# Sliding-window attention and an S4 convolution: x read flat and first, pools on two sides with waits by tile, projections dealt over the real table steps, the kernel's transform beside the first maxima

## The chip, the core and the metric

One core of one Trainium2 chip runs the whole program. The metric is the time of one execution on the device in microseconds (us); the time of a kernel is the median of its runs. The engines are PE (matrix multiplication, with PEld for its weight loads), DVE (vector), ACT (activation functions), POOL (the second vector-like engine) and SP, which here only issues DMA transfers. Each engine runs its own list of instructions in order and waits on semaphores for the others.

## What is computed

```python
def _A_ref(x, wqkv, wo):              # x 1x2048x576, 32 heads of 18
    qkv = (x @ wqkv).reshape(B, S, 3, H, Dh).transpose(2, 0, 3, 1, 4)
    q, k, v = qkv[0], qkv[1], qkv[2]
    scores = einsum("bhqd,bhkd->bhqk", q, k) * Dh ** -0.5
    scores = where(0 <= i - j < 256, scores, -1e9)
    o = einsum("bhqk,bhkd->bhqd", softmax(scores), v)
    return o.transpose(0, 2, 1, 3).reshape(B, S, D) @ wo

def _B_ref(u, A_re, A_im, B_re, B_im, C_re, C_im, log_dt, Dskip):
    P = exp(dt * A * l)               # 576 channels, 128 states, l = 0..2047
    K = einsum("dn,dnl,dn->dl", Cc, P, dB).real
    return causal_convolution(u, K) + u * Dskip

out = concatenate([_A_ref(...), _B_ref(...)], axis=-1)
```

## The kernel before

Two independent halves share the engines. Their work is cut into generators, and `merge` takes from several of them in proportion to the numbers given with them.

**Up to the seam** the Tile framework orders the instructions by itself, from the order in which they are written. `proj` first reads x in eight pieces of 512 KB and the weights `wqkv` in four, for the largest absolute value of each (`amax`), which sets a power-of-two scale. Then it cuts the weights into two float16 parts (`wh`, `wl`), reads x a second time in four chunks of 512 tokens, cuts each likewise (`xh`, `xl`), and makes 13 steps per chunk: nine blocks of q and k (14 matmuls of 512 columns each, evicted to `qst` and stored to the DRAM tensor `qd`) and four steps of v (28 matmuls of 288 columns, stored to `vd`). With the steps for loads and weights that is 16 and 56 steps. All projection matmuls carry line 172 in the profile of before.

`s4_prep` multiplies the S4 parameters by dt and splits two of them into three bfloat16 parts each (`split3`). `tables` builds the convolution kernel K (64 x 128 x 144 values) in 36 half-steps of 16 channels: exponentials (`mg`, `mab`), sines (`fraction`, `qtable`), products on POOL (`m`), and then the taps, 128 small matmuls into `kp` (line 418), evicted to K every second half-step (line 424, 18 times). It has 308 steps after the first 20. `s1_u` is the first stage of the convolution's transform for u, 16 blocks, each stored to `gx` in two transfers of 288 KB (matmuls on line 461, evictions on lines 128 and 130 by `evac`, three of four on ACT and the fourth on DVE).

**The seam.** When all of this is done, `s1_k` runs the same first stage over K: eight blocks of 1152 columns, each stored to `gk` in two transfers of 576 KB, from two buffers `g1`. Then the pools of the second half are opened, `att_setup` clears the operand sets on DVE, and two units of Q and K are loaded.

**After the seam** the order is written out by hand (`manual_schedule`). `attention` first makes the row maxima of unit 0 (`gmax(0)`, 19 steps, matmuls on line 636, maxima on line 643), together with six steps of the convolution `conv`. The maxima go back by a small DMA (`Q<-mt`), and then come 96 items: scores (line 677), exponentials (line 679), masks on POOL (line 688), values (line 700), with the maxima of the next unit, steps of `conv` (95 over the 76 items from the third on, 17 over the next 16), and later the output projection (line 903). `conv` starts with the load of its first operands (`tx` from `gx`, `tk` from `gk`); its matmuls are on lines 500 and 508. SP's queue takes nearly all loads and stores, in order.

## Time and profile before

| | |
|---|---|
| times of the runs | 1076.2, 1079.5, 1081.78 us, median 1079.5 |
| the profiled execution | 1075.61 us, its span 1073.6 us |
| PE busy | 857.8 us, 80% of the span |
| DVE busy | 736.2 us, 69% |
| ACT busy | 619.9 us, 58% |
| POOL busy | 511.1 us, 48% |
| moved by DMA | 152.27 MB, mean 142 GB/s |

The span runs from the first to the last instruction. A row of the profile for a group of instructions gives the source line, the engine, the operation, what it writes and reads by the program's names, the shapes and the count, then the busy time in us and the mean ns of one, and then the engine's idle time before these instructions with what ended most of it. In a row of the timeline the first number is the start in us from the start of the span and the second the duration; the brackets behind it hold the idle time before and what ended it. A matmul of float32 operands leaves two records per instruction.

### The profile page before, as it was taken

Reading aid. Unit: us, or ns where it says so; the run is one execution under the profiler, and the core shown is the slowest. Engines: PE = TensorE matmul, PEld = TensorE weight load, DVE = VectorE, ACT = ScalarE, POOL = GpSimd, SP = SyncE. Lnnn points to the kernel's source line nnn. Section 1 sums busy time; section 2 is a strip of 40 time slices with the busy share of each in tenths; the row PEclk is TensorE's granted clock in tenths of the full one; section 3 lists DMA queues with packets and bytes.
Section 4 is the critical chain, followed back from the end, with each engine's and each line's share of the span. In section 5 each row is a group of like instructions: output and inputs, shape, how many; then the busy total and the mean of one; then the engine's idle time right before and its main releaser. Section 6 shows DMA issues by size and latency. Waiting matters only on the chain.

```text
span 1073.6 us, 26801 instructions
## 1 busy us (share of the span) xinstructions
PE 857.8 (80%) x10332; PEld 450.7 (42%) x10332; DVE 736.2 (69%) x1859; ACT 619.9 (58%) x955; POOL 511.1 (48%) x606
## 2 busy tenths in 40 slices
PE   1535879897988797987578888878888899988787
PEld 0313436554744464553234333333333344434345
DVE  2879685669576845226676788888878766767564
ACT  1776758776797784233146655566566656644471
POOL 0004344435452632010235677766876666666770
PEclk9966989998998998999889999999999999999999
DMA  9665423442344232588616456454645644579763
GB/s 271 168 184 160 105 53 88 109 94 59 85 111 96 55 74 64 130 217 239 188 49 180 138 147 175 147 148 127 176 113 177 185 118 142 146 185 256 204 190 121
DMA packets 155911, 152.27 MB, mean 142 GB/s; under 512 B 36856, under 2 KB 134392, under 8 KB 155592
## 3 DMA queue, kind: packets, MB, share of 16 engines
q1 hardware_dynamic: 148152, 131.98, 45.3%
q0 software_dynamic: 6128, 14.60, 5.4%
q10 hardware_dynamic: 1504, 3.99, 1.3%
q8 instruction: 81, 1.33, 0.6%
q14 instruction: 46, 0.38, 0.1%
HBM read 89.12 MB, written 61.01 MB: 140 GB/s over the span
## 4 chain that ended last, share of the span: by engine, by line
PE 37%; DVE 25%; ACT 10%; DMA 10%; issue 9%; POOL 5%; SPq 2%; DVEq 0%; ACTq 0%; POOLq 0%
PE pp L172 8%; PE r L636 4%; PE po L700 4%; PE r L903 4%; PE r L500 4%; PE kp L418 4%; PE pp L461 3%; DVE jk L643 3%; POOL P L688 2%; DMA gk<-g 2%; PE ST L677 2%; PE x L314 2%; PE r L508 2%; DVE tr L358 2%; ACT P L679 2%
## 5 line engine op out<-in xcount | busy, mean ns | idle before, releaser
L643 DVE CUSTOM_DVE_ANT_0 jk<-r,bias 128x288 f32<-128x288 f32 (+7 forms) x512 | 198.0, 433 | 88.7 <-PE r L636 88.0
L679 ACT ACTIVATE P<-ST,esc 128x1024 f32<-128x1024 f32 (+1 forms) x192 | 202.0, 1059 | 92.9 <-PE ST L677 92.1
L380 POOL TENSOR_TENSOR m<-A,tr 128x1024 f32<-128x1024 f32 x72 | 149.5, 2098 | 194.2 <-PE kp L418 139.1
L688 POOL TENSOR_SCALAR_AFFINE_SELECT P<-P 128x512 f32<-128x512 f32 x240 | 171.7, 745 | 103.2 <-ACT P L679 100.8
L636 PE MATMUL r<-K,qb 128*64 128x288 f16 (+7 forms) x1024 | 130.5, 297 | 36.7 <-DVE qb L627 10.7
L700 PE MATMUL po<-P,V 128*32 128x256 f32 (+2 forms) x1408 | 100.2, 395 | 17.5 <-POOL P L688 8.1
L418 PE MATMUL kp<-Q,m 128*32 128x64 f32 x4608 | 88.3, 230 | 27.6 <-DVE Q L401 10.0
L636 PEld LDWEIGHTS <-qb 128*64 128x64 f16 x1024 | 60.3, 109 | 119.3 <-issue 65.6
L536 POOL TENSOR_TENSOR Y<-t,t 64x288 f32<-64x288 f32 x64 | 53.5, 835 | 109.8 <-DVE t L531 107.8
L418 PEld LDWEIGHTS kp<-Q,m 128*32 128x32 f32 x4608 | 75.2, 116 | 56.3 <-issue 41.7
L461 PE MATMUL pp<-ut,w 128*128 128x288 f32 x128 | 52.8, 538 | 40.9 <-DMA ut<-in_u_dram 18.6
L677 PE MATMUL ST<-Q,K 64*128 64x384 f16 (+2 forms) x704 | 73.5, 280 | 3.0 <-DMA Q<-mt 2.9
L237 DVE SCALAR_TENSOR_TENSOR qst<-pp,qst 128x512 f16<-128x512 f32 x36 | 24.7, 685 | 64.7 <-ACT qst L236 61.8
L128 ACT ACTIVATE g<-pp 128x288 f32<-128x288 f32 (+1 forms) x84 | 34.5, 447 | 40.4 <-DMA gk<-g 22.0
L700 PEld LDWEIGHTS po<-P,V 128*32 128x32 f32 x1408 | 35.7, 110 | 52.5 <-issue 25.7
L537 POOL TENSOR_TENSOR Y<-t,t 64x288 f32<-64x288 f32 x64 | 54.5, 852 | 3.8
L461 PEld LDWEIGHTS pp<-ut,w 128*128 128x128 f32 x128 | 28.9, 245 | 61.1 <-issue 24.1
L326 ACT ACTIVATE ab<-k 128x512 f32<-128x512 f32 (+1 forms) x54 | 31.9, 590 | 37.0 <-DVE k L325 36.6
L172 PE MATMUL pp<-xh,wh 128*128 128x512 f16 x180 | 47.9, 388 | 1.2 <-DVE xh L229 1.2
L172 PEld LDWEIGHTS <-wh 128*128 128x128 f16 x324 | 32.0, 101 | 39.3 <-issue 6.6
L172 PE MATMUL pp<-xh,wl 128*128 128x512 f16 x180 | 48.3, 392 | 0.0
L500 PE MATMUL r<-tx,w 128*64 128x288 f32 x256 | 40.2, 430 | 9.9 <-DMA tx<-gx 8.7
(177 smaller groups left out, 1756.1 us busy)
## 6 DMA issues: line engine op xcount, KB each, us to landing
gx<-g SPq DMA_DIRECT2D x32, 288.0 KB
qd<-qst SPq DMA_DIRECT2D x72, 128.0 KB
gk<-g SPq DMA_DIRECT2D x16, 576.0 KB
tx<-gx SPq DMA_DIRECT2D x16, 576.0 KB
tk<-gk SPq DMA_DIRECT2D x16, 576.0 KB
h<-ho SPq DMA_DIRECT2D x16, 576.0 KB
raw<-in_xT_dram SPq DMA_DIRECT2D x16, 512.0 KB
Q<-qd SPq DMA_DIRECT2D x32, 216.0 KB
```

Of the source, the lines that this page charges most:

```text
L172: self.nc.tensor.matmul(ps, u, v, start=(i == 0), stop=(i == len(ops) - 1))
L380: self.nc.gpsimd.tensor_tensor(m, A[:, ch, a0:a0 + 8].unsqueeze(3).to_broadcast(sh), tr[:, ch, part, 0:8].unsqueeze(2).to_broadcast(sh), o ...
L418: nc.tensor.matmul(kp[32 * st:32 * st + 32, c % 2 * JJ2 + j, :], m[:, ch, a0:a0 + 32], Q[:, ch, term % 2, :], start=(term == 0), stop=(ter ...
L461: nc.tensor.matmul(ps, self.w1[:, part, :], src[:, o:o + k], start=True, stop=True)
L500: nc.tensor.matmul(ps[64 * par:64 * par + 64], w2[:, par, 64 * part:64 * part + 64], t[:, 2 * hs:2 * hs + 2, par, :], start=True, stop=True)
L537: nc.gpsimd.tensor_tensor(Y[par][64:128], t1[sl, 1], t2[sl, 1], op=OP.add)
L636: nc.tensor.matmul(ps[64 * b:64 * b + 64, :n], self.qb[:, b, t, :], d["K"][:, b, k0:k0 + n], start=True, stop=True, skip_group_check=True)
L643: nc.vector.tensor_tensor_reduce(out=jk[:, :n], in0=ps[:, :n], in1=self.bias[:, 288 - n:], scale=1.0, scalar=-3e38, op0=OP.add, op1=OP.max ...
L677: nc.tensor.matmul(ps[:, u, o:o + n], d["K"][h, jp, k0:k0 + 128], d["Q"][h, jp, q0:q0 + n], start=True, stop=True, skip_group_check=True)
L679: nc.scalar.activation(pt[:, 2 * jp:2 * jp + 2, lo:hi], ps[:, :, lo:hi], AF.Exp, scale=self.esc)
L688: nc.gpsimd.affine_select(v, v, pattern=[[0, 4], [sg, 128]], compare_op=OP.is_ge, fill=0.0, base=-1 if far else 0, channel_multiplier=-sg)
L700: nc.tensor.matmul(self.po[32 * j:32 * j + 32, t0 * 128:t1 * 128], V[:, kb * 76 + 19 * j:kb * 76 + 19 * j + 32], pt[:, j, o:o + (t1 - t0) ...
```

## The change

Five things, at these places:

- `proj` reads x for its maximum as one flat array, 128 partitions of contiguous rows, in four pieces of 2160 columns and one of 576, into the buffers that later hold `wh`, `wl` and `qst`. These reads and the four of the weights, with their nine maxima, are now its first step, and `build` takes that step before `s4_prep`.
- `pool` places each on-chip pool on a side (left by default, right for K, `s1s`, `pps` and the pools of `proj` and `s1_u`), and asks for waits by tile (`reuse_waits="tile"`) where memory is used again.
- The projections are merged against 308 table steps instead of 400; the first merge takes four projection, 16 table and two u steps.
- `s1_k` makes 16 blocks of 576 columns instead of eight of 1152. Ten are written out with the first half, six beside `gmax(0)`, before the pools of the second half are opened.
- `conv` gives way once after its first load, which is issued in the first item; the six steps that ran beside `gmax(0)` join the others: 101 over the 76 items.

```diff
--- before.py
+++ after.py
@@ -118,8 +118,10 @@
             if d[0] <= n:
                 d[1](*d[2])
 
-    def pool(self, es, name, bufs, space=None):
+    def pool(self, es, name, bufs, space=None, side="left"):
         kw = {} if space is None else {"space": space}
+        if space != DRAM:
+            kw.update(side=side, reuse_waits="tile")
         self.p[name] = es.enter_context(self.tc.tile_pool(name=name, bufs=bufs, **kw))
 
     def evac(self, out, in_):
@@ -159,7 +161,7 @@
         return self.pow2_of(self.pow2_max(parts, nm)[1], nm)
 
     def amax(self, out, v):
-        self.nc.vector.tensor_reduce(out, v, axis=AX.XY, op=OP.max, apply_absolute_value=True)
+        self.nc.vector.tensor_reduce(out, v, axis=AX.XY if len(v.shape) > 2 else AX.X, op=OP.max, apply_absolute_value=True)
 
     def mm14(self, ps, w, x, wsl, xsl, flip=False):
         wh, wl = w
@@ -183,21 +185,25 @@
         nc, a, wp, dp, sp = self.nc, self.a, self.p["wq"], self.p["dram"], self.p["const"]
         self.qd = dp.tile([64 * 54 + 18, L], F16, name="qd")
         self.vd = dp.tile([8, 128, 16, 76], F32, name="vd")
-        amx = sp.tile([128, 12], F32, name="amx")
+        amx = sp.tile([128, 9], F32, name="amx")
         wr = self.p["K"].tile([128, 5, 1728], F32, name="K")
-        for c in range(8):
-            t = self.p["raw"].tile([128, 5, 256], F32, name="raw")
-            self.load_rows(t, a["xT"], slice(c * 256, c * 256 + 256))
-            self.amax(amx[:, c:c + 1], t)
-            if c % 2 == 0:
-                cs = slice(c // 2 * 432, c // 2 * 432 + 432)
-                self.load_rows(wr[:, :, cs], a["wqkv"], cs)
-            yield
+        flat = a["xT"].rearrange("r c -> (r c)").rearrange("(p n) -> p n", p=128)
+        for i, nm in enumerate(("wh", "wl")):
+            t = wp.tile([128, 4320], F32, name=nm)
+            for c in range(2):
+                o = 2160 * (2 * i + c)
+                nc.sync.dma_start(t[:, 2160 * c:2160 * c + 2160], flat[:, o:o + 2160])
+                self.amax(amx[:, 2 * i + c:2 * i + c + 1], t[:, 2160 * c:2160 * c + 2160])
+        t = self.p["pst"].tile([128, 576], F32, name="qst")
+        nc.sync.dma_start(t, flat[:, 8640:])
+        self.amax(amx[:, 4:5], t)
         for c in range(4):
-            self.amax(amx[:, 8 + c:9 + c], wr[:, :, c * 432:c * 432 + 432])
-            yield
-        px, self.sx = self.pow2_scale(amx[:, 0:8], "x")
-        pw, self.sw = self.pow2_scale(amx[:, 8:12], "w")
+            cs = slice(c * 432, c * 432 + 432)
+            self.load_rows(wr[:, :, cs], a["wqkv"], cs)
+            self.amax(amx[:, 5 + c:6 + c], wr[:, :, cs])
+        yield
+        px, self.sx = self.pow2_scale(amx[:, 0:5], "x")
+        pw, self.sw = self.pow2_scale(amx[:, 5:9], "w")
         pz = self.pz = sp.tile([128, 1], F32, name="pz")
         self.esc = sp.tile([128, 1], F32, name="esc")
         nc.vector.scalar_tensor_tensor(pz, px, 0.25, pw, op0=OP.mult, op1=OP.mult)
@@ -471,10 +477,10 @@
             self.s1(ut.rearrange("p l j -> p (l j)"), self.gx, l0, 4, "pps")
             yield
 
-    def s1_k(self):
+    def s1_k(self, pp):
         kf = self.K.rearrange("p l j -> p (l j)")
-        for b in range(8):
-            self.s1(kf[:, b * 1152:(b + 1) * 1152], self.gk, 8 * b, 8, "s1p")
+        for b in range(16):
+            self.s1(kf[:, b * 576:(b + 1) * 576], self.gk, 4 * b, 4, pp[0])
             yield
 
     def conv(self):
@@ -513,6 +519,7 @@
                 self.after(1, nc.sync.dma_start, self.h.rearrange("a l f d -> (a l) f d")[:, 2 * fp:2 * fp + 2, :], ho)
 
         nx = load(0)
+        yield
         last = None
         for fp in range(16):
             cu = nx
@@ -766,18 +773,21 @@
             nc.gpsimd.dma_start(self.od[:, f0:f0 + 18, HQ * hf:HQ * hf + HQ].rearrange("a p n -> p a n"),
                                 h[32 * j:32 * j + 18])
 
-    def attention(self, conv):
-
-
-        self.V, self.Pt, self.osb, self.ops, self.hl, norms = {}, {}, {}, {}, {}, []
+    def attention_start(self):
+        self.V, self.Pt, self.osb, self.ops, self.hl = {}, {}, {}, {}, {}
         self.load_unit(0)
         self.load_unit(1)
-        merge((self.gmax(0), 19), (part(conv, 6), 6))
-        self.begin(1)
+
+    def attention(self, conv):
+
+
+        norms = []
         items = [(i, c, b) for i in range(16) for c in range(2) for b in range(3)]
         wo0, wo1, wo2, wl, self.acc, self.h7 = self.wo_first(), self.wo_part(), self.wo_rest(2), self.wo_load(), [], {}
         for n in range(len(items) + 2):
             self.begin(n)
+            if n == 0:
+                next(conv)
             streams = []
             if n < len(items):
                 i, k = n // 6, n % 6
@@ -804,7 +814,7 @@
                     streams.append((part(gm, g), g))
             if n >= 2:
                 streams.append((self.values(*items[n - 2]), 1))
-                k = share(n - 2, 95, 76) if n < 78 else share(n - 78, 16, 17) if n < 95 else 0
+                k = share(n - 2, 101, 76) if n < 78 else share(n - 78, 16, 17) if n < 95 else 0
                 streams.append((part(conv, k), k))
             if 20 <= n < 52 and n % 2 == 0:
                 next(wl, 0)
@@ -952,39 +962,46 @@
             self.gx = dp.tile([2, 64, 128, 144], F32, name="gx")
             self.gk = dp.tile([2, 64, 128, 144], F32, name="gk")
             self.h = dp.tile([2, 64, 32, D], F32, name="h")
-            with ExitStack() as ek:
-                self.pool(ek, "K", 1)
-                with ExitStack() as e1:
-                    for n, b, s in (("s4c", 1, None), ("pps", 3, PSUM), ("xps", 2, PSUM), ("trig", 1, PSUM),
-                                    ("kps", 1, PSUM)):
-                        self.pool(e1, n, b, s)
-                    with ExitStack() as e2:
-                        self.pool(e2, "prep", 1)
-                        self.s4_prep()
-                    for n, b in (("wq", 1), ("raw", 2), ("x", 1), ("pst", 2), ("s1u", 2), ("s1s", 2), ("ab", 2), ("abt", 1), ("mab", 3),
-                                 ("mg", 4), ("fr", 2), ("Q", 2), ("P", 2)):
-                        self.pool(e1, n, b)
-                    proj, tables, s1u = self.proj(), self.tables(), self.s1_u()
-                    merge((part(proj, 16), 16), (part(tables, 20), 20), (part(s1u, 4), 4))
-                    merge((proj, 56), (tables, 400), (s1u, 12))
-                with ExitStack() as e1:
-                    self.pool(e1, "s1s", 2)
-                    self.pool(e1, "s1p", 3, PSUM)
-                    for _ in self.s1_k():
-                        pass
+            ek, e0 = ExitStack(), ExitStack()
+            self.pool(ek, "K", 1, side="right")
+            self.pool(ek, "s1s", 2, side="right")
+            self.pool(ek, "pps", 3, PSUM, side="right")
+            pp = ["pps"]
+            s1k = self.s1_k(pp)
             with ExitStack() as e1:
-                self.pool(e1, "fc", 1)
+                for n, b in (("s1u", 2), ("wq", 1), ("raw", 2), ("x", 1), ("pst", 2)):
+                    self.pool(e1, n, b, side="right")
+                for n, b, s in (("s4c", 1, None), ("xps", 2, PSUM), ("trig", 1, PSUM), ("kps", 1, PSUM)):
+                    self.pool(e1, n, b, s)
+                proj, tables, s1u = self.proj(), self.tables(), self.s1_u()
+                next(proj)
+                with ExitStack() as e2:
+                    self.pool(e2, "prep", 1)
+                    self.s4_prep()
+                for n, b in (("ab", 2), ("abt", 1), ("mab", 3), ("mg", 4), ("fr", 2), ("Q", 2), ("P", 2)):
+                    self.pool(e1, n, b)
+                merge((part(proj, 4), 4), (part(tables, 16), 16), (part(s1u, 2), 2))
+                merge((proj, 56), (tables, 308), (s1u, 14))
+                for _ in part(s1k, 10):
+                    pass
+            for n, b, s in (("att", 1, None), ("m", 2, None), ("v", 4, None), ("ring", 3, PSUM)):
+                self.pool(e0, n, b, s)
+            self.att_setup()
+            with self.tc.manual_schedule():
+                self.attention_start()
+                merge((self.gmax(0), 19), (s1k, 6))
+                self.begin(1)
+                ek.close()
+                for n, b, s in (("P", 4, None), ("o", 3, None), ("n", 2, None), ("n1", 1, None), ("h7", 1, None),
+                                ("wo", 1, None), ("wo2", 2, None),
+                                ("fc", 1, None), ("fs", 2, None), ("fy", 2, None), ("stp", 2, PSUM), ("ops", 1, PSUM)):
+                    self.pool(e0, n, b, s)
                 self.i2 = self.p["fc"].tile([128, 64], F32, name="i2")
                 nc.sync.dma_start(self.i2, a["c_i2"])
                 self.dsk = self.p["fc"].tile([128, D], F32, name="dsk")
                 nc.sync.dma_start(self.dsk, a["dsk"].partition_broadcast(128))
-                for n, b, s in (("fs", 2, None), ("fy", 2, None), ("att", 1, None), ("m", 2, None), ("P", 4, None),
-                                ("v", 4, None), ("o", 3, None), ("n", 2, None), ("n1", 1, None), ("h7", 1, None), ("wo", 1, None), ("wo2", 2, None),
-                                ("stp", 2, PSUM), ("ops", 1, PSUM), ("ring", 3, PSUM)):
-                    self.pool(e1, n, b, s)
-                self.att_setup()
-                with self.tc.manual_schedule():
-                    self.attention(self.conv())
+                self.attention(self.conv())
+            e0.close()
 
 
 def kernel(**inputs):
```

The lists of instructions are as follows. On DVE, at the program's start, before (`nA_re` is the first S4 operand, `amx` a maximum, `res` the rest of a split):

```order
L288 MEMSET halfpi 128x1
L162 TENSOR_REDUCE amx<-K 128x1 x2
L292 TENSOR_TENSOR nA_re<-nA_re,dtn 96x2304
L294 SCALAR_TENSOR_TENSOR nA_im<-nA_im,dtn 96x2304
L261 TENSOR_TENSOR res<-nA_re,al 96x2304
L298 TENSOR_TENSOR in_B_re<-in_B_re,dt 128x576
```

and now (`wh`, `wl` and `qst` hold pieces of x here):

```order
L294 MEMSET halfpi 128x1
L164 TENSOR_REDUCE amx<-wh 128x1 x2
L164 TENSOR_REDUCE amx<-wl 128x1 x2
L164 TENSOR_REDUCE amx<-qst 128x1
L298 TENSOR_TENSOR nA_re<-nA_re,dtn 96x2304
L164 TENSOR_REDUCE amx<-K 128x1
L267 TENSOR_TENSOR res<-nA_re,al 96x2304
```

The five maxima of x stand ahead of the first S4 operation, and the four over K are spread between the operations of the first split, the last two ahead of its second half.

On PE, at the seam, before (`pp` a projection or first-stage result, `r` with `tx` the convolution's second stage, `r` with `qb` the maxima):

```order
L172 MATMUL pp<-wh,xl 128x288
L172 LDWEIGHTS xl
L172 MATMUL pp<-wh,xl 128x288
L461 MATMUL pp<-K,w_62 128x384 x48
L500 MATMUL r<-tx,w_6125 64x288 x4
L636 LDWEIGHTS qb
L636 MATMUL r<-K_6085,qb 64x32
```

and now:

```order
L424 MATMUL kp<-Q,m_5537 32x64 x8
L424 MATMUL kp<-Q,m_5539 32x64 x8
L467 MATMUL pp<-K,w_62 128x288 x44
L643 LDWEIGHTS qb
L643 MATMUL r<-K_5991,qb 64x32
```

Before, the last taps were followed by 238 projection matmuls and eight of u, and the whole of K's first stage came before the first `r`. Now the last taps stand directly ahead of K's first stage, 44 of whose 64 matmuls (eleven blocks) come before the first maxima; the other five blocks stand between them, four matmuls after every twelve. Over the whole first half 56 projection matmuls now stand ahead of the first taps and 896 between the first and the last, where 714 stood; of u's 64 it is 13 ahead and 51 between, where it was 20, 36 and eight behind.

## The prediction

> **What bounds the kernel now.** I read the times first, then busy time by stretch, then single lines inside the stretches, then the chain of waits at the seams. The page shows no engine above 80% of the span, so the limit has to be looked for by stage. The row of each stretch gives its length, then for each engine the busy time and the number of instructions, the granted TensorE clock, the DMA share and GB/s:
>
> ```profile
> core 0: us, PE busy (x) PEld busy (x) DVE busy (x) ACT busy (x) POOL busy (x), PEclk, DMA share, GB/s
> 0.00:27.00 27.00, 4.54 (x8) 2.35 (x8) 7.32 (x5) 2.96 (x6) 0.91 (x5) 1.00 0.97 271
> 27.00:49.00 22.00, 13.60 (x28) 7.41 (x29) 20.09 (x18) 16.25 (x16) 0.00 (x0) 1.00 0.71 191
> 49.00:91.00 42.00, 12.88 (x34) 4.99 (x32) 33.74 (x40) 31.71 (x41) 9.94 (x7) 0.64 0.62 180
> 91.00:420.00 329.00, 276.64 (x5526) 171.46 (x5527) 230.59 (x347) 242.85 (x412) 141.47 (x69) 0.92 0.36 85
> 420.00:467.70 47.70, 46.00 (x269) 26.06 (x257) 7.12 (x11) 11.72 (x24) 1.45 (x4) 1.00 0.59 131
> 467.70:515.00 47.30, 35.59 (x96) 17.61 (x96) 27.88 (x28) 16.36 (x36) 3.51 (x1) 0.96 0.84 239
> 515.00:543.50 28.50, 16.09 (x109) 7.76 (x110) 19.14 (x79) 4.57 (x9) 6.93 (x10) 0.80 0.47 141
> 543.50:1073.60 530.10, 452.50 (x4278) 213.02 (x4277) 390.31 (x1336) 293.52 (x412) 346.89 (x510) 0.98 0.56 158
> ```
>
> Until 27 us the DMA engines are full. From 27 to 91 DVE and ACT prepare the tables. From 91 to 420, the table stretch, PE is busy for 276.6 of 329 us. From 420 to 467.7 PE works almost alone. To 515 the kernel K goes through its first transform and out to HBM, with DMA at 0.84. Up to 543.5 the first maxima run with six steps of the convolution, and then the attention items start, with PE at 85%.
>
> Who works alone from 420 on is seen from line 172 (projections) and then line 461 (first transforms) in the two stretches:
>
> ```profile
> 91.00:420.00 329.00, 143.22 (x714) 70.11 (x714) 0.92 0.36 85
> 420.00:467.70 47.70, 41.57 (x238) 23.21 (x238) 1.00 0.59 131
> ```
>
> ```profile
> 91.00:420.00 329.00, 25.74 (x72) 14.23 (x72) 0.92 0.36 85
> 420.00:467.70 47.70, 4.75 (x17) 2.78 (x17) 1.00 0.59 131
> ```
>
> A quarter of the projection (238 of 952 matmuls) is left when the tables end: `merge` dealt 56 projection steps against 400 table steps, and the tables have 308.
>
> **The change part by part.** The sum is made on the profiled execution: 1075.6 us around a span of 1073.6. That is 3.9 us under the median of the runs shown, so the same difference is put on the median of 1079.5 at the end.
>
> *The tail goes.* The built order has no projection behind the last taps. The last eviction of K and its predecessors stand here (first and last start):
>
> ```profile
> L424 ACT ACTIVATE K<-kp x18: 1016/1032/1063, 102.9 to 420.3; 128x512 f32<-128x512 f32 x18
> ```
>
> From 420.3 to 467.7 is 47.4 us. Term: -47.4.
>
> *The work comes back inside the tables.* By the built order 896 projection matmuls now stand between first and last taps instead of 714, 56 stand ahead (free: PE idles for 29 of the 42 us before 91), and 51 first-transform matmuls of u instead of 36, at two records each. At the tail's prices that adds 182 x 41.57/238 = 31.8 us and 30 x 4.75/17 = 8.4 us, so 316.8 us of PE in a stretch that was 329 long. It fits, but only at 96%. How dense PE gets there:
>
> ```profile
> 170.00:209.40 39.40, 37.91 (x803) 25.74 (x800) 27.21 (x45) 34.06 (x65) 19.72 (x11) 1.00 0.48 119
> 209.40:222.60 13.20, 9.33 (x212) 6.30 (x213) 11.63 (x20) 6.08 (x12) 5.51 (x3) 0.74 0.24 52
> 275.20:327.90 52.70, 48.46 (x1155) 32.08 (x1156) 39.68 (x63) 43.45 (x78) 29.45 (x14) 1.00 0.39 96
> ```
>
> Over 40 us it reaches 96%, over 53 us 92%; I take 92%, the longer one: 316.8/0.92 = 344, term +15. Ends: 0 if all of it is hidden in the 52 us of PE idle time, -13 if the clock helps as well, +56 if none of the waits shrinks (both worked out as rivals).
>
> The middle row has PE at 9.3 of 13.2 us and a granted clock of 0.74; its dense neighbours have 1.00. Over the whole stretch 0.92 stands for some 53 us at half speed. The Trainium skill (TensorE: Matmul & The Clock Gate, HAM oscillation) says that PE idle gaps beyond about 3.4 us let the clock fall to half; by that rule a fuller stretch would lose such spells, and the term would be -13 (rival e).
>
> *x first.* x is now read once flat, ahead of everything on SP's queue, and once more in pieces for the transform's operands. ACT's own loads run beside it, and their rows and those of the table's start are:
>
> ```profile
> 22.31 0.62 ACTq L286 DMA_DIRECT2D in_C_im<-in_p_C_im_dram  x1
> 22.97 1.28 ACT L289 ACT_TABLE_LOAD   x1 [22.97 <-DMA dt<-in_ldt_dram]
> 24.51 2.56 DVE L292 TENSOR_TENSOR nA_re<-nA_re,dtn 96x2304 f32<-96x2304 f32 x1
> 47.78 2.39 DVE L162 TENSOR_REDUCE amx<-K 128x1 f32<-128x2160 f32 x1
> 71.08 0.55 DVE L325 TENSOR_TENSOR k<-x,k 128x384 f32<-128x384 f32 x1
> ```
>
> ```profile
> q10 hardware_dynamic: 1504, 3.99, 1.3%
> ```
>
> x is 576 x 2048 x 4 bytes = 4.72 MB; with ACT's 3.99 MB (q10), 8.7 MB at the first row's 271 GB/s are in at 32 us, and DVE's `nA_re`, now queued behind five maxima of x, starts there instead of at 24.5. The weights (4.42 MB) follow until 48.5, so the last maximum over K is where it was, 47.8. But behind it in line now stand what used to run earlier (the second halves of both splits, four products by dt) and what came later (four weight conversions, two of x, evictions). By these rows the waiting ACT and DVE pieces are:
>
> ```profile
> L162 DVE TENSOR_REDUCE amx<-raw 128x1 f32<-128x1280 f32 x7 | 10.3, 1480 | 1.1 <-DMA raw<-in_xT_dram 0.9
> L209 ACT ACTIVATE wh<-K,wr 128x2160 f16<-128x2160 f32 x4 | 8.4, 2091 | 0.0
> L264 DVE TENSOR_TENSOR res<-res,al 32x2304 f32<-32x2304 f32 x1 | 2.5, 2550 | 0.5 <-ACT al L263 0.5
> ```
>
> ```profile
> 31.93 0.75 DVE L298 TENSOR_TENSOR in_B_re<-in_B_re,dt 128x576 f32<-128x576 f32 x1
> ```
>
> After 51: 8.1 us on DVE (2.55 + 2.5 for the second split + 3.0 for the products), then on ACT two conversions of that split, one more, and four of weights (3 x 2.1 + 4 x 2.1 = 14.7), some 9 of small evictions, and 2.7 for x: the first fraction k comes near 86 instead of 71.1. From there to the first taps, which the chain has at 91.28, the old order needed 20.2 us, of which five maxima of x (7.4) and one weight pass (2.5) are gone: 86 + 10.3 = 96. Term +5, with +1 for projections now in ACT's line: +6. Ends: -4 (the 9.9 us of removed maxima and weight pass as pure gain, less 6 for x landing later) and +20 (a rival).
>
> ```profile
> 91.28 3.43 PE kp L418 x120
> ```
>
> *The seam.* K's first transform is now 16 blocks with stores of 288 KB instead of 8 with 576 KB, still in two buffers. How long a buffer is held, one eviction pair of u, the wait for tx, the maxima, and the wait for their result:
>
> ```profile
> 473.58 0.37 SPq L463 DMA_DIRECT2D gk<-g  x1
> ...
> 477.18 0.87 ACT L128 ACTIVATE g<-pp 128x384 f32<-128x384 f32 x2 [2.09 <-DMA gk<-g]
> ```
>
> ```profile
> 450.28 0.90 ACT L128 ACTIVATE g<-pp 128x288 f32<-128x288 f32 x2 [1.47 <-PE pp L461]
> ```
>
> ```profile
> 515.26 6.09 DMA tx<-gx
> ...
> 542.33 1.72 DMA Q<-mt
> ```
>
> ```profile
> L643 DVE CUSTOM_DVE_ANT_0 jk<-r,bias 128x288 f32<-128x288 f32 (+8 forms) x32 | 11.5, 416 | 8.1 <-PE r L636 8.1
> ```
>
> The large store holds its buffer for 3.6 us. Half of it lies between 1.8 and 3.6; I take 2.9, nearer the whole one since issue and receipt do not shrink. With 0.9 for the evictions and 0.3 for waits a block takes 4.1 us. Eleven blocks come before the maxima, and five stand between them, where DVE's six maxima a block (6 x 0.42 = 2.5) fit. From the last eviction of K: 15 x 4.1 = 61.5, 4.6 for both ends, 2 for the result's way back: 68 instead of 75.8 (467.7 to 543.5). The tx wait of 6 us and the six convolution steps leave this place. Term -8; ends -24 (3.0 a block) and +3 (4.8). The Trainium skill (DMA: Bandwidth & Descriptors, Anatomy of one DMA) gives, for transfers that GpSimd starts, about 2.0 us plus size over 436 GB/s, 2.7 us here by estimate; by that the block would be 3.9.
>
> *The convolution's six steps.* They go into the item loop (101 steps over 76 items, where 95 were):
>
> ```profile
> 543.50:959.00 415.50, 73.95 (x472) 26.61 (x472) 0.99 0.53 149
> ```
>
> ```profile
> 543.50:959.00 415.50, 40.62 (x124) 20.08 (x124) 0.99 0.53 149
> ```
>
> These are line 500 (16 records per column half) and line 508 (4 per half): 2.5 + 1.3 = 3.8 us of PE a half, and six steps are two halves, 7.6 us. At PE's 85% I count 6. Ends: 0, and +26 if every step stretches the loop in proportion (6/95 of 415).
>
> *Pools on two sides, waits by tile.* No instruction of its own; they let the maxima's tiles be opened while K stands on the other side. Where a wait stays, it is in the terms above. Their cover is the stores' pace; without the two sides the maxima would start after all 16 blocks, 5 x 4.1 = 20 us later, with 12 of their own to follow.
>
> Sum: -47.4 + 15 + 6 - 8 + 6 = -28. 1075.6 - 28 = 1047.6, and on the median 1051.5, say **1052 us**.
>
> **Rivals.** (a) *PE's idle time takes all of the projection*: the stretch stays 329, term 0, total -43, 1036. For it: 52 us idle. Against: 96% was held for 40 us only. (e) *The fuller stretch also keeps its clock*: without 53 us at half speed up to 26 us of PE work go, 291/0.92 = 316, term -13, total -56, 1024. For it: 1.00 in both dense rows. Against: spells come after waits for Q and m too, which stay. (b) *PE becomes the line in which the tables queue*: taps stand behind whole projection columns in PE's order, DVE and POOL wait for Q's and m's two buffers, so the idle share stays as it is. Place: the table stretch. Price: the added records at the stretch's own prices (182 x 143.22/714 = 36.5, 30 x 25.74/72 = 10.7) at 276.6/329 = 84%: 323.8/0.84 = 385, +56, total +13, 1092: slower. It decides from a stretch of about 372 us on (43 more), where the gain is gone. Against it: PE reaches 92% and more where it has work. (c) *Small stores cost as much as large ones*: eight pairs took 46.8 us, 5.85 a pair; 15 x 5.85 + 6.6 = 94, a seam 18 longer than before, total -2, 1078: no change. Against: half the bytes at 0.84 DMA share. (d) *x in front stalls the tables' start* by 20 us instead of 6 (first taps at 111): -14, 1066. For it: DMA at 0.97 until 27, and the whole split chain behind the weights' last maximum. The Trainium skill (DMA: Bandwidth & Descriptors, Issuing engines are not separate DMA queues) says that loads of both queues share the same 16 engines, which is what the 32 us above assume.
>
> **How the numbers follow.** Forecast 0.52; (a) 0.10, (b) 0.15, (c) 0.08, (d) 0.10, (e) 0.05. The range from 1030 to 1082 holds (a), (c), (d) and the forecast's own 1033 to 1071, and leaves out (b) and (e). 0.5%, 5.4 us, is about what a measurement can tell from no change. Faster than that: the forecast but for its edge, (a), (e) and most of (d): 0.74. Within: (c) and edges: 0.10. Slower: (b) and a remainder: 0.16.
>
> **What would show it.** Right: no projection behind the last eviction of K; that eviction near 441, the first one near 109; PE above 90% between; 4 us from one small store to the next but one; the first score matmul near 509; the item loop about 6 us longer. Wrong: 360 us or more from first to last eviction of K (b), more than 5 us a block (c), first taps after 105 (d), or a loop longer by 20 us.

## The result, and the profile after

The changed kernel takes 1078.6 us (median of 20 runs, 1077.0 to 1082.0) and the kernel before 1079.3 (20 runs): ratio 0.9997, 95% interval 0.9986 to 1.0009. The change made no difference that can be measured, where 1052 was forecast. The profiled execution of the change has a span of 1075.2 us, that of before 1073.6, so the terms can be compared one by one. Here are the stretches of the changed kernel (length, then busy time and number of instructions of each engine, granted clock, DMA share, GB/s). The cuts that matter are the first taps (104.7), the first and the last eviction of K (112.1 and 461.3) and the first score matmul (530.1):

```profile
core 0: us, PE busy (x) PEld busy (x) DVE busy (x) ACT busy (x) POOL busy (x), PEclk, DMA share, GB/s
...
49.00:78.00 29.00, 10.50 (x25) 5.36 (x25) 26.40 (x32) 24.36 (x24) 1.47 (x2) 0.62 0.31 84
78.00:104.70 26.70, 18.43 (x77) 7.76 (x76) 15.48 (x26) 17.91 (x33) 8.41 (x4) 0.82 0.47 122
104.70:112.10 7.40, 7.40 (x260) 6.57 (x261) 7.40 (x12) 4.77 (x10) 3.96 (x2) 0.61 0.21 44
112.10:461.30 349.20, 306.05 (x5488) 188.37 (x5486) 223.37 (x339) 257.32 (x434) 139.31 (x74) 0.95 0.40 94
461.30:504.30 43.00, 31.16 (x90) 18.49 (x92) 23.26 (x24) 13.40 (x33) 0.00 (x0) 0.84 0.64 189
504.30:530.10 25.80, 19.41 (x106) 11.58 (x106) 15.46 (x74) 7.85 (x17) 0.00 (x0) 0.93 0.47 139
```

The events are read from the rows of the instructions themselves, first and last start: the evictions of K, and the stores of K's first transform.

```profile
L430 ACT ACTIVATE K<-kp x18: 1012/1038/1057, 112.1 to 461.3; 128x512 f32<-128x512 f32 x18
```

```profile
L469 SPq DMA_DIRECT2D gk<-g x32: 359/360/458, 465.2 to 527.1; - x32
```

The first score matmul starts at 530.1. For the kernel before, the same length of the table stretch is

```profile
102.90:420.30 317.40, 267.75 (x5273) 164.63 (x5272) 220.68 (x327) 235.52 (x403) 140.75 (x68) 0.93 0.36 85
```

| term | forecast | measured | from |
|---|---|---|---|
| projection tail | -47.4 | -47.4 | nothing of line 174 behind 461.3 |
| first to last eviction of K | +15 | +31.8 | 349.2 - 317.4 |
| first eviction of K | +6 | +9.2 | 112.1 - 102.9 |
| seam to the first score matmul | -8 | -7.0 | (530.1 - 461.3) - 75.8 |
| item loop | +6 | +15.0 | (1075.2 - 530.1) - 530.1 |
| sum | -28 | +1.6 | 1075.2 - 1073.6 |

The tail went as forecast. What it freed was given back in the tables (17 us more than forecast), the loop (9) and the front (3). PE's work in the stretch rose by 306.05 - 267.75 = 38.3 us, about the forecast 40, but PE is busy for 88% of the stretch and not for 92%.

The loop, for both kernels cut at the first score matmul, the 4th and the 26th eviction of `osb` (32 in all), before and then after:

```profile
543.50:609.00 65.50, 57.54 (x530) 25.74 (x531) 47.72 (x211) 36.80 (x53) 38.92 (x55) 0.96 0.43 118
609.00:950.90 341.90, 297.40 (x2847) 135.49 (x2846) 271.40 (x948) 205.50 (x293) 238.67 (x339) 1.00 0.55 154
950.90:1073.60 122.70, 97.56 (x906) 51.78 (x904) 71.19 (x179) 51.22 (x68) 69.29 (x117) 0.96 0.68 188
```

```profile
530.10:597.10 67.00, 57.81 (x536) 26.03 (x535) 48.45 (x211) 36.72 (x53) 35.91 (x54) 0.95 0.51 147
597.10:956.00 358.90, 305.50 (x2886) 139.55 (x2882) 276.15 (x956) 207.50 (x301) 242.40 (x347) 0.99 0.52 149
956.00:1075.20 119.20, 96.62 (x906) 51.62 (x904) 71.27 (x179) 51.11 (x68) 69.50 (x117) 0.96 0.69 196
```

The middle part grew by 17.0 us with 8.1 us more of PE work. One jump of 5 us in it is seen in the chain of waits of the changed kernel:

```profile
713.45 13.19 DMA raw<-in_wo_dram
726.70 0.76 issue
727.46 1.10 ACT P L686
```

A piece of wo, issued behind the loads of a unit and of the convolution, lands 13.2 us later; ACT's conversion of it (line 876) waits for 3.2 us, and the exponentials of the item stand behind that in ACT's order. Whether this is what the loop lost is tested below.

### The profile page after: what moved, and what is told of

Same layout as the page of the kernel before. It is cut to its first block, busy times and chain, and to the rows that moved or that the text cites. A ratio compares the mean times of both kernels' runs of the same rounds, so it can differ in the third digit from the quotient of the medians.

```text
span 1075.2 us, 26897 instructions
## 1 busy us (share of the span) xinstructions
PE 856.7 (80%) x10364; PEld 457.9 (43%) x10364; DVE 734.9 (68%) x1860; ACT 631.9 (59%) x975; POOL 503.0 (47%) x606
## 4 chain that ended last, share of the span: by engine, by line
PE 39%; DVE 21%; DMA 12%; ACT 12%; issue 9%; SPq 3%; POOL 3%; DVEq 0%; ACTq 0%; POOLq 0%
PE pp L174 8%; PE r L643 5%; PE po L707 4%; PE pp L467 4%; PE r L913 4%; PE kp L424 3%; PE r L506 3%; PE r L514 3%; PE ST L684 3%; DVE jk L650 2%; PE x L320 2%; DMA c_ca<-in_c_ca_dram 2%; DMA gk<-g 1%; DMA K<-in_wqkv_dram 1%; POOL P L695 1%
## 5 line engine op out<-in xcount | busy, mean ns | idle before, releaser
L386 POOL TENSOR_TENSOR m<-A,tr 128x1024 f32<-128x1024 f32 x72 | 146.3, 2054 | 250.2 <-PE kp L424 182.5
L695 POOL TENSOR_SCALAR_AFFINE_SELECT P<-P 128x512 f32<-128x512 f32 x240 | 166.1, 722 | 161.7 <-ACT P L686 159.2
L643 PE MATMUL r<-K,qb 128*64 128x288 f16 (+7 forms) x1024 | 129.8, 296 | 41.7 <-DVE t L537 11.5
L467 PE MATMUL pp<-ut,w 128*128 128x288 f32 x128 | 47.2, 494 | 57.8 <-DMA ut<-in_u_dram 45.2
L130 ACT ACTIVATE g<-pp 128x288 f32<-128x288 f32 x96 | 37.3, 411 | 50.7 <-PE pp L467 25.7
L467 PEld LDWEIGHTS pp<-ut,w 128*128 128x128 f32 x128 | 26.7, 225 | 70.8 <-issue 45.6
L467 PE MATMUL pp<-K,w 128*128 128x288 f32 x128 | 43.9, 492 | 11.9 <-ACT g L130 10.7
L174 PEld LDWEIGHTS <-wh 128*128 128x128 f16 x324 | 32.1, 101 | 49.2 <-issue 17.8
L132 DVE COPY g<-pp 128x288 f32<-128x288 f32 x32 | 14.6, 456 | 56.2 <-PE pp L467 47.1
```

Of the source, the lines that this page charges most:

```text
L174: self.nc.tensor.matmul(ps, u, v, start=(i == 0), stop=(i == len(ops) - 1))
L386: self.nc.gpsimd.tensor_tensor(m, A[:, ch, a0:a0 + 8].unsqueeze(3).to_broadcast(sh), tr[:, ch, part, 0:8].unsqueeze(2).to_broadcast(sh), o ...
L467: nc.tensor.matmul(ps, self.w1[:, part, :], src[:, o:o + k], start=True, stop=True)
L643: nc.tensor.matmul(ps[64 * b:64 * b + 64, :n], self.qb[:, b, t, :], d["K"][:, b, k0:k0 + n], start=True, stop=True, skip_group_check=True)
L695: nc.gpsimd.affine_select(v, v, pattern=[[0, 4], [sg, 128]], compare_op=OP.is_ge, fill=0.0, base=-1 if far else 0, channel_multiplier=-sg)
```

## The experiments

**Which part does what.** First the dealing alone, in the kernel before:

```diff
-                    merge((proj, 56), (tables, 400), (s1u, 12))
+                    merge((proj, 56), (tables, 304), (s1u, 12))
```

> The kernel before with one number changed: the projections are dealt over the 304 table steps that really remain, nothing else. Before: first to last eviction of K 102.9 to 420.3 (317.4), then 47.4 us of projection. After the whole change: 349.2 and nothing behind. Theory 'the dealing moves the tail into the tables at most of its price': no projection behind the last eviction of K, the stretch grows by about 32 us to some 349, the seam and the item loop stay as before, so the time falls by about 15 us, to some 1064. Rival 'it is the other parts of the change (x first, waits by tile) that made the tables slower': the stretch grows by about 15 us as I had forecast, time about 1047. Rival 'the tail comes back whole': stretch 365, no change.

Measured: 1066.6 us, ratio to before 0.9905 (0.9877 to 0.9933). The stretch in its profile:

```profile
103.20:457.10 353.90, 311.32 (x5529) 188.55 (x5527) 229.22 (x341) 258.99 (x435) 140.82 (x73) 0.96 0.40 95
```

353.9 us, 36.5 more than before, so 11 of the 47.4 us are won; the loop stays (531.1). The first theory is the nearest: it had 349 us and 1064, and the growth is 4.6 us above it. One number was worth 11 us, and the other parts of the change took that away.

Then the six convolution steps alone, moved in the kernel before:

```diff
         nx = load(0)
+        yield
...
-        merge((self.gmax(0), 19), (part(conv, 6), 6))
+        next(conv)
+        merge((self.gmax(0), 19))
...
-                k = share(n - 2, 95, 76) if n < 78 else share(n - 78, 16, 17) if n < 95 else 0
+                k = share(n - 2, 101, 76) if n < 78 else share(n - 78, 16, 17) if n < 95 else 0
```

> The kernel before, with the six convolution steps taken out of the first maxima (only the first load of the convolution stays there) and dealt into the item loop, 101 steps over 76 items instead of 95. Theory 'the six steps are worth 6 to 9 us in the loop': first score matmul to the end 530.1 grows to some 537 to 539; the first score matmul comes 5 us or more earlier than 543.5 because the wait for tx and the six steps leave that place, total about as before, 1077 to 1082. Rival 'the loop's whole growth of 15 us comes with the six steps': 545. Rival 'the loop grew for another reason (a late load of wo, buffers in other places) and the six steps cost nothing': 530 and the whole about 5 us faster.

Measured: 1088.3 us, ratio 1.0094 (1.0059 to 1.0129), 0.9% slower. The first score matmul comes at 536.7, 6.8 earlier, but the loop takes 551.1, 21 more, with the growth in the same place:

```profile
536.70:605.40 68.70, 60.43 (x537) 26.78 (x538) 48.62 (x211) 37.96 (x54) 35.96 (x54) 0.91 0.40 118
605.40:965.50 360.10, 307.49 (x2886) 140.64 (x2882) 275.91 (x956) 207.98 (x302) 242.59 (x347) 0.98 0.51 149
```

The first rival holds: the loop's whole growth comes with these steps. Third, the changed kernel with the front of before. The expectation speaks of x alone (eight pieces again), but the edit also puts back the first deal's numbers, 16, 20 and 4, then 304 and 12:

```diff
-        flat = a["xT"].rearrange("r c -> (r c)").rearrange("(p n) -> p n", p=128)
...
+        for c in range(8):
+            t = self.p["raw"].tile([128, 5, 256], F32, name="raw")
+            self.load_rows(t, a["xT"], slice(c * 256, c * 256 + 256))
...
-                next(proj)
...
-                merge((part(proj, 4), 4), (part(tables, 16), 16), (part(s1u, 2), 2))
-                merge((proj, 56), (tables, 308), (s1u, 14))
+                merge((part(proj, 16), 16), (part(tables, 20), 20), (part(s1u, 4), 4))
+                merge((proj, 56), (tables, 304), (s1u, 12))
```

> The changed kernel with x read as the kernel before reads it (eight pieces of 256 columns, each fourth part of the weights between them, behind the tables' own preparation in the program), all else as changed. Changed kernel: first K eviction at 112.1 (before: 102.9), 349.2 us from first to last. Theory 'reading x flat and first costs the tables' start 9 us': first eviction near 103, the stretch unchanged within 4 us, time some 9 us lower, about 1069. Rival 'what the front loses it gives back in the stretch, since the projection's operands are ready earlier and 56 projection matmuls stand ahead of it': first eviction near 103 and a stretch of some 357, no change. Rival 'the later start comes from the pools and the program order, not from x': first eviction stays near 112, no change.

Measured: 1065.6 us, ratio 0.9887 (0.9856 to 0.9917). First taps 103.2 and first eviction 109.0, only 1.5 and 3.1 us earlier, but the stretch is 341.1 instead of 349.2:

```profile
109.00:450.10 341.10, 304.00 (x5492) 185.37 (x5490) 227.06 (x340) 255.46 (x432) 137.62 (x74) 0.95 0.40 93
```

No theory had this: most of the gain lies in the stretch. To part x from the numbers, the numbers alone:

```diff
-                merge((part(proj, 4), 4), (part(tables, 16), 16), (part(s1u, 2), 2))
-                merge((proj, 56), (tables, 308), (s1u, 14))
+                merge((part(proj, 4), 4), (part(tables, 20), 20), (part(s1u, 4), 4))
+                merge((proj, 56), (tables, 304), (s1u, 12))
```

> The changed kernel with only the numbers of the first deal put back: 20 table steps and 4 of u's first transforms ahead, then 304 and 12 (changed: 16 and 2, then 308 and 14); x stays flat and first. So far: changed, first K eviction 112.1, stretch 349.3; x in pieces with the old numbers, 109.0 and 341.1, 13 us faster. Theory 'the two blocks of u that now stand ahead of the tables make most of the shorter stretch' (two blocks are 16 records of 0.28 us, 4.5 us of PE): stretch about 344, time about 1074. Rival 'reading x in pieces among the weights makes it': stretch 349, no change. Rival 'the numbers make all of it': 341, time about 1066.

Measured: 1070.4 us, ratio 0.9934 (0.9903 to 0.9964).

```profile
113.40:453.80 340.40, 296.20 (x5476) 183.03 (x5474) 227.88 (x340) 254.07 (x431) 138.44 (x74) 0.96 0.39 94
```

The stretch is 340.4: the numbers make all of the 8 us in it. In five other profiles with the changed kernel's front (the runs on the loop and the seam) it is 346.4 to 348.7. Reading x flat itself seems to cost 3.7 us at the last eviction of K (453.8 against 450.1). But that event moves by 5 us between profiles with one and the same front (456.2 to 461.3), and the intervals of the two ratios overlap, so a cost of x itself is not shown.

**The loop.** Two edits of the changed kernel. The first takes the loads of wo out of the items in which a unit is loaded, the second deals the six steps one each to items 2 to 7 and goes on as before:

```diff
-            if 20 <= n < 52 and n % 2 == 0:
+            if 21 <= n < 53 and n % 2 == 1:
```

> The changed kernel, with the steps that load and convert wo taken in odd items (21 to 51) instead of even ones (20 to 50), so that its seventh load (issued at 713.45 behind the loads of a unit and of the convolution, 13.2 us to landing) no longer stands behind a unit's loads in the same item. Theory 'the late load holds ACT and with it one item': the jump of 5.5 us between 722.8 and 743.3 goes, first score matmul to the end 545.1 falls to about 540, time about 1073.5. Rival 'the stall only moves what the loop would wait for anyway': 545, no change.

```diff
-                k = share(n - 2, 101, 76) if n < 78 else share(n - 78, 16, 17) if n < 95 else 0
+                k = share(n - 2, 95, 76) + (n < 8) if n < 78 else share(n - 78, 16, 17) if n < 95 else 0
```

> The changed kernel with the six further convolution steps dealt one each to the first six items that take convolution steps (n = 2 to 7), and from there on 95 over 76 as in the kernel before, so that the later loads of the convolution fall on the same items as before. So far: first score matmul to the end 530.1 (before), 545.2 (changed), 551.1 (the kernel before with 101 over 76). Theory 'it is not the work of the six steps but where the thinner deal puts the convolution's loads and steps against a unit's loads, the maxima and the load of wo': the loop comes to 536 to 540, the jump near the 13th output chunk (202.0 after the first score before, 213.2 in the changed kernel) goes, time about 1071. Rival 'each step stretches the loop in proportion, about 3 us a step': 545 to 551, no change.

Measured: the first 1079.1 us, ratio 1.0022 (0.9994 to 1.0050), its loop 553.0. ACT's wait for wo is gone from its trace, but nothing is won (5 us would have been a ratio near 0.995): the rival holds. The second 1066.5 us, ratio 0.9910 (0.9876 to 0.9945):

```profile
522.00:597.20 75.20, 65.23 (x574) 28.93 (x575) 52.19 (x219) 40.07 (x62) 45.12 (x63) 0.93 0.51 147
597.20:941.70 344.50, 299.93 (x2846) 136.28 (x2844) 269.07 (x948) 205.59 (x293) 240.05 (x338) 0.99 0.54 152
```

The steps cost 9.7 us in the first stretch (75.2 against 65.5), and the middle one is back at 344.5. Over the profiles of this study, those told of below too, the loop takes 530 to 534 us with 95 steps (3 kernels), 537 to 540 with six more at the start (4), and 545 to 553 with 101 over 76 (11). By their means (531.6, 538.7, 549.0) the steps themselves cost some 7 us, near the forecast 6, and the thin deal some 10 more. Profiles of the same loop differ by up to 8 us (545 to 553), so the 15.0 of the change and the 21 of the steps alone are one price, and one pair of profiles says little: between the changed kernel and the second edit only 5.5 us of difference lie in the loop (545.1, 539.6).

**The seam.** The maxima behind the stores; three store buffers; large blocks with a buffer of their own, the last three beside the maxima:

```diff
-                merge((self.gmax(0), 19), (s1k, 6))
+                merge((s1k, 6))
+                merge((self.gmax(0), 19))
```

> The changed kernel with the first maxima behind all of K's first transform instead of beside its last six blocks. In the kernel before without convolution steps there the maxima alone took 13.9 us (522.8 to 536.7). Theory 'the overlap hides the maxima': last eviction of K to first score matmul 68.7 grows by 10 to 14, to 79 to 83. Rival 'the maxima slow the stores as much as they are hidden': 68 to 72.

```diff
-            self.pool(ek, "s1s", 2, side="right")
+            self.pool(ek, "s1s", 3, side="right")
```

> The changed kernel with three buffers instead of two for the first transforms' rows on their way out (1152 KB in two stores of 288 KB a block, two blocks' worth of waiting behind one another). So far: 15 blocks in 61.9 us (465.2 to 527.1), 4.1 a block; DMA share 0.53 between 461 and 531. Theory 'the stores' round trip sets the pace, not their bytes': about 2.9 us a block, the last eviction of K to the first score matmul falls from 68.7 to some 52 to 56, time 12 us lower, about 1066. Rival 'the bytes or the evictions set it': 66 or more, no change.

```diff
-        for b in range(16):
-            self.s1(kf[:, b * 576:(b + 1) * 576], self.gk, 4 * b, 4, pp[0])
+        for b in range(8):
+            self.s1(kf[:, b * 1152:(b + 1) * 1152], self.gk, 8 * b, 8, pp[0])
...
-                for _ in part(s1k, 10):
-                    pass
+            self.pool(ek, "s1s", 2, side="right")
+            for _ in part(s1k, 5):
+                pass
...
-                merge((self.gmax(0), 19), (s1k, 6))
+                merge((self.gmax(0), 19), (s1k, 3))
```

> The changed kernel with K's first transform again in 8 blocks of 1152 columns and stores of 576 KB (in a buffer of its own on the other side), the last three of them, instead of the last six small ones, beside the first maxima. So far: 8 large blocks took 46.8 us before, 16 small ones 61.9 to 65.6; last eviction of K to first score matmul 75.8 before (with six convolution steps in it), 67.9 in the kernel before without these steps, 68.7 changed. Theory 'the overlap with the maxima gained some 14 to 20 us and the small stores gave it back': the seam falls to 54 to 58, time about 1066. Rival 'the maxima beside the stores cost what they save, whatever the size': 66 to 70, no change.

Measured, from the last eviction of K to the first score matmul: maxima last 77.2 (461.1 to 538.3; one run, 1089.0 us); three buffers 63.2 (1073.3 us, ratio 0.9971, 0.9955 to 0.9987); large blocks 63.9 (1075.0 us, ratio 0.9981, 0.9957 to 1.0005). The stores of K's transform in four profiles, first the dealing alone (large, with the old seam), then maxima last, three buffers, large beside the maxima:

```profile
L463 SPq DMA_DIRECT2D gk<-g x16: 359/360/388, 462.5 to 504.6; - x16
```

```profile
L469 SPq DMA_DIRECT2D gk<-g x32: 359/360/459, 464.7 to 523.1; - x32
```

```profile
L469 SPq DMA_DIRECT2D gk<-g x32: 359/360/616, 462.3 to 519.7; - x32
```

```profile
L469 SPq DMA_DIRECT2D gk<-g x16: 359/360/521, 466.5 to 519.3; - x16
```

Read from the first store's issue to the last one's, large stores alone take 42.1 us (42 to 46 in the four profiles with the old seam), small ones 58.4, small ones beside maxima 61.9. So the small size costs some 16 us for the same bytes where the maxima come later; beside the maxima, with little else changed, it costs 9 (61.9 against 52.8). Behind the last store the first score matmul came 29.8 us later with the old seam (534.4), 15.2 with the maxima alone (538.3) and 3.0 in the changed kernel. The first step, 14.6, belongs to the convolution steps and the wait for tx that left: taken out of the kernel before, they took the 29.3 us there to 17.8, which is 11.5 of it. The second, 12.2, is the overlap, less the 3.5 by which it slows the stores. Against the dealing alone, +16.3 - 14.6 - 8.7 = -7.0, and 1.5 for an earlier first store, make the whole seam 68.8 instead of 77.3; that the table's -7.0, against 75.8, is the same number is chance. These shares are one way of taking the sum apart: the profiles with the old and the new seam differ in more than one thing.

A third buffer takes 4.5 us off the stores and 5.6 off the seam, which lies between the theory (52 to 56) and its rival (66 or more); large blocks beside the maxima gain 5 and not 12.

**What fills the table stretch.** Half sums instead of whole ones, so that fewer projection matmuls stand ahead of a table's:

```diff
+            if i == 6:
+                yield
...
-                self.mm14(ps, (wh, wl), (xh, xl), slice(m * 128, m * 128 + 128), slice(0, 512))
+                yield from self.mm14(ps, (wh, wl), (xh, xl), slice(m * 128, m * 128 + 128), slice(0, 512))
...
-                merge((proj, 56), (tables, 308), (s1u, 14))
+                merge((proj, 124), (tables, 308), (s1u, 14))
```

> The changed kernel with each projection sum of 14 matmuls dealt in two halves of 7 (124 steps over the 308 table steps instead of 56), so that table matmuls stand behind 7 projection matmuls at most. So far: stretch from first to last K eviction 349.3, PE busy 306.1 in it (88%), idle 43. Theory 'the tables' waits behind whole sums keep PE's idle time': idle falls to some 30, the stretch to about 336, time about 1066. Rival 'PE's idle time comes from ACT, DVE and POOL (Q, m, kp), whatever the grain': 347 to 351, no change.

Measured: 1077.5 us, ratio 0.9998 (0.9984 to 1.0012), stretch 347.6: the rival holds, the grain does not matter.

```profile
112.70:460.30 347.60, 305.40 (x5488) 186.09 (x5486) 219.60 (x338) 256.53 (x435) 134.57 (x70) 0.94 0.39 93
```

Then with products left out, so that only the times mean anything (one execution each):

```diff
-        ops = [(wh, xh, k) for k in range(5)] + [(wl, xh, k) for k in range(5)] + [(wh, xl, k) for k in range(4)]
+        ops = [(wh, xh, k) for k in range(5)] + [(wh, xl, k) for k in range(4)]
```

> The changed kernel with the five products of the weights' low halves left out of every projection sum (9 of 14 matmuls stay; 320 fewer among the 896 of the table stretch, at 143.22/714 some 64 us of PE). The kernel before put 182 fewer there and was 32 us shorter. Theory 'the stretch follows PE's work at 0.83 us per us added': 349 - 53 = about 296. Rival 'the tables' own chain of ACT, DVE and POOL has a floor near before's 317': 312 to 320. If PE alone set it: 285.

```diff
-        ops = [(wh, xh, k) for k in range(5)] + [(wl, xh, k) for k in range(5)] + [(wh, xl, k) for k in range(4)]
+        ops = [(wh, xh, 0)]
```

> The changed kernel with 13 of the 14 products left out of every projection sum (one matmul a sum stays; evictions, splits and stores as they are). So far, PE busy in the stretch from first to last K eviction and its length: 306.1 and 349.3 whole, 253.3 and 310.4 with 9 of 14. Here PE's work falls to some 306 - 832 x 0.2 = 140. Theory 'the tables have a length of their own, and only PE work above about 250 us shows': stretch 295 to 310. Rival 'the stretch follows PE's work at 0.74 us per us': 310 - 0.74 x 113 = 226.

The stretch with 9 products, and with one:

```profile
112.20:422.60 310.40, 253.27 (x5164) 158.09 (x5163) 223.00 (x337) 249.14 (x430) 139.34 (x71) 0.93 0.43 101
```

```profile
112.10:417.60 305.50, 204.84 (x4647) 126.38 (x4647) 216.99 (x336) 247.34 (x428) 141.49 (x74) 0.79 0.44 106
```

310.4 us with 9 of 14, 305.5 with one. The first is just under the rival's 312 to 320 and well above the theory's 296; the second is in the range of its theory (295 to 310), far from 226. The projection matmuls alone, in the same stretch with one product, with nine, in the kernel before and in the changed one:

```profile
112.10:417.60 305.50, 20.23 (x61) 5.78 (x61) 0.79 0.44 106
112.20:422.60 310.40, 121.01 (x576) 56.36 (x576) 0.93 0.43 101
102.90:420.30 317.40, 142.03 (x711) 69.50 (x710) 0.93 0.36 85
112.10:461.30 349.20, 173.68 (x896) 88.89 (x896) 0.95 0.40 94
```

From 20 to 121 us of projection the stretch grows by 5 us, from there to 142 by 7, and the last 32 us make it 32 longer (the kernel before has another front and fewer blocks of u). So the tables have a length of their own, and projection that no longer fits beside it is added to it. The 305 us are an upper end for that length, since the clock fell to 0.79 in the run with one product (see the last section). The chain of waits through the stretch agrees: projection matmuls make 16.1% of it before (51 us) and 22.7% in the changed kernel (79 us), 28 of the 31.8 us.

**The tables' start.** Waits by tile alone, in the kernel before with the new deal:

```diff
+        if space != DRAM:
+            kw.update(reuse_waits="tile")
```

> The kernel before with the deal over 304 steps (1066.6 so far) and with waits by tile in all its pools on chip, which stay on one side and in their old order. Theory 'waits by tile let the projection's operands be made ahead of the tables' and so hold the tables' start': first taps near 103 instead of 89.8, first projection matmul near 90 instead of 102.5. Rival 'it is the projection's pools on the other side, free from the beginning, that do this': first taps near 90, and no change against 1066.

Measured: first taps 90.1, 1069.1 us (0.9918, 0.9892 to 0.9944), as without it (89.8, 0.9905): waits by tile do nothing there. In the fastest kernel (next), the projection's pools back on the tables' side and behind their preparation:

```diff
-                for n, b in (("s1u", 2), ("wq", 1), ("raw", 2), ("x", 1), ("pst", 2)):
-                    self.pool(e1, n, b, side="right")
...
-                proj, tables, s1u = self.proj(), self.tables(), self.s1_u()
...
-                for n, b in (("ab", 2), ("abt", 1), ("mab", 3), ("mg", 4), ("fr", 2), ("Q", 2), ("P", 2)):
+                for n, b in (("s1u", 2), ("wq", 1), ("raw", 2), ("x", 1), ("pst", 2), ("ab", 2), ("abt", 1), ("mab", 3), ("mg", 4), ("fr", 2), ("Q", 2), ("P", 2)):
...
+                proj, tables, s1u = self.proj(), self.tables(), self.s1_u()
```

> The fastest so far (x in pieces, six convolution steps in items 2 to 7, 8 large blocks beside the maxima; 1052.0; first taps 103.1, last K eviction 448.1) with the projection's five pools again on the tables' side and opened behind the tables' preparation, as before. Theory 'the pools' place decides the tables' start': first taps near 90, first projection matmul near 102, last K eviction 445 to 455 because the projections then stand later; time 1049 to 1058. Rival 'the pools have no part in it': first taps 103 and 1052.

Measured: first taps 99.7 instead of 103.1, last eviction of K 450.3 instead of 448.1, 1056.5 us (0.9806, 0.9768 to 0.9844). The pools' place is worth 3.4 us at the start, little more than the 3 us by which first taps differ between profiles with one front. What holds the other 10 against 90 no run parts. The trace only shows where they lie: with the pools back, the first fraction of a sine (line 327 there) is at 62.4, earlier than the 71.1 of the kernel before. But then the second halves of the weights (`wl`, line 212) keep DVE until 91.7, where they ended at 74.0 before, and the first `Q` follows at 97.9. The earlier start was not worth having either: two projection sums instead of three stood ahead of the first eviction.

**A kernel that beats both**: x in pieces with the old first deal, the six steps early, large blocks beside the maxima (the edits shown above, together), and a variant of it with more of u ahead:

> Changed kernel with three edits at once: x in pieces as before (1065.6 alone), the six convolution steps one each in items 2 to 7 (1066.5 alone, loop 539.5), and 8 large blocks in K's first transform beside the maxima. If they add: 1078.6 - 13 - 12 - 12 = about 1042; if the large blocks bring nothing, 1053; if x and the convolution steps overlap in what they save, 1058 or more.

```diff
-                merge((part(proj, 16), 16), (part(tables, 20), 20), (part(s1u, 4), 4))
-                merge((proj, 56), (tables, 304), (s1u, 12))
+                merge((part(proj, 16), 16), (part(tables, 20), 20), (part(s1u, 8), 8))
+                merge((proj, 56), (tables, 304), (s1u, 8))
```

> The fastest so far (1052.0, stretch 339.2) with eight instead of four of u's sixteen first transforms dealt ahead of the tables (8 instead of 12 behind). Theory 'PE is idle before the first taps, so u's blocks there cost nothing and four blocks fewer shorten the stretch by 4 x 8 x 0.36 = 11 us at PE's price': stretch 328 to 332, first eviction at most 2 later, time about 1044. Rival 'their loads and evictions hold the tables' start on ACT and DVE by as much': first eviction 6 or more later, no change.

Measured: the first 1052.0 us, ratio 0.9757 (0.9715 to 0.9800); the variant 1061.0 (0.9843, 0.9806 to 0.9881). Stretch, seam and loop of the first:

```profile
108.90:448.10 339.20, 301.28 (x5490) 184.57 (x5487) 227.06 (x340) 254.78 (x431) 137.61 (x74) 0.96 0.40 94
448.10:508.20 60.10, 45.35 (x161) 22.04 (x162) 38.09 (x94) 19.00 (x38) 0.00 (x0) 0.94 0.68 196
508.20:1047.70 539.50, 461.88 (x4322) 216.62 (x4321) 393.15 (x1344) 296.85 (x420) 352.41 (x518) 0.97 0.57 161
```

The edits nearly add, each at what it measured alone: 1078.6 - 13.0 - 12.1 - 3.6 = 1049.9, 2 us below the measured time. The 1042 of the expectation counted 12 for the large blocks, and whether their 3.6 is in the sum these times cannot tell. In the variant the first eviction of K moves from 108.9 to 122.9 and the stretch falls only to 335.3. That is the rival's side, and worse than its "no change": 9 us are lost. The first taps start only 4.1 us later (107.2); why the rest of the way to the first eviction takes 10 more no run parts.

## Why the prediction was wrong, point by point

- **The tail** (-47.4) was right: it went to the last matmul, and the dealing alone shows that its going was worth 11 us net.
- **The stretch** is the step that failed most: "Over 40 us it reaches 96%, over 53 us 92%; I take 92%, the longer one". The work to be put in was right (38 us against 40). Its density was taken from the two fullest pieces of the stretch, as if the waits in between were room. The runs show that they were not: PE is busy for 88%, the tables take 305 us with one projection product of 14 (some 290 by the estimate in the last section), and the last 32 us of projection cost 32 (of the last 53 us of all PE work, from 253.3 to 306.1, 39 show as time). The measured +31.8 lies between the +15 of 92% and the +46 that 38.3 us would cost at the stretch's own 84%. Rival (b), PE's busy share staying at 84%, fell too (88%, and 349 is under its 372). Its mechanism fell only in part: half sums changed nothing, so the grain is not it, but the chain does show the projections in the tables' line.
- **x first**: +9 instead of +6 at the first eviction. The first fraction is at 86.8, as forecast (86), with 19 projection matmuls on PE among the products ahead of it. From there to the first tap it took 17.9 us and not 10.3:

```profile
78.59 0.85 PE pp L174 x2
...
82.01 1.51 PE pp L174 x4
...
84.82 1.08 PE pp L174 x5
86.30 0.50 ACT k L330
86.82 0.57 DVE k L331
```

  Taking five maxima of x and a weight pass off DVE was counted as 9.9 us saved of 20.2 on this way. It was 19.1, since the first tap stood at 90.2 (91.28 is a later piece of the chain), and it shrank by 1.2. The rows of this way, first before and then after, suggest why:

```profile
71.10:90.20 19.10, 3.22 (x11) 0.77 (x11) 18.04 (x26) 12.09 (x20) 8.41 (x4) 0.50 0.74 221
86.80:104.70 17.90, 9.63 (x48) 4.28 (x47) 13.38 (x22) 14.06 (x25) 8.41 (x4) 0.88 0.44 106
```

  DVE has 4.7 us less to do, and it is no longer the fuller engine: ACT is busy for 14.1 of the 17.9 us. So most of what left DVE was no time off the way. Rival (d), 20 us for x in front, came near in size (14.5 at the first taps), but not in its cause: with x in pieces again they are at 103.2 instead of 104.7. What makes the rest of the delay stays open. Not seen at all was that the first deal's new numbers (two blocks of u and four table steps fewer ahead) cost 9 us in the stretch (349.2 against 340.4).
- **The seam** was right in sum (-7.0 for -8) and in its pace: 61.9 us for 15.5 blocks is 4.0 a block. The sum is partly luck: the saving comes from the steps that left, while the smaller stores lose 9 to 16 us and the overlap wins about 9. The prediction added up the new seam as a whole and did not see these parts.
- **The six steps**: "six steps are two halves, 7.6 us. At PE's 85% I count 6". At 85% the 7.6 would be 8.9; the 6 is not worked out. Dealt early the steps cost about 7. The deal over 76 items costs some 17. The upper end of 26 was in the text; the likely value was taken from the work and not from where the other steps land. The wait for wo, which the chain names, is not the cause: without it the loop was no shorter. Which meeting of steps and loads costs the 10 us stays open.
- **(c), (d), (e)**: a small block takes 4.0 us and not 5.85; first taps at 104.7 are just under the 105 of (d); the clock did rise in the stretch, from 0.93 to 0.95, and the stretch grew all the same.

## What to carry to other kernels

Before work is moved into another engine's waits, ask how long that stretch would be without it: leave the work out in two or three steps and look, with an eye on the granted clock. A stretch's fullest pieces tell what the engine can do, not what its waits leave free. And steps taken into a loop should be put where the rest of the loop keeps its places: six steps early cost 7 us, and the same six spread thin over 76 items cost 17.
